# Warming products, the order of small ACT and PE steps, and units of four columns in a fused dynamic convolution and maxout kernel

## The chip, the cores and the metric

The kernel runs on one core of a Trainium2 chip (trn2). The metric is the device time of one execution in microseconds (us). Engines are named as the profile names them: PE is TensorE (PEld its weight loads), DVE is VectorE, ACT is ScalarE, POOL is GpSimd, and SP is SyncE, which only issues DMAs here. Median of four runs before the change: 415.58 us (415.46 to 415.68).

## The reference

```python
# dynamic convolution: batch 8, sequence 4160, 192 channels, 8 heads, 7 taps
w = exp(weight_gen - max); w = w / (sum(w) + 1e-9)      # over the 7 taps
x_unf = x padded by 6 zeros in front, 7 shifted views, split into heads
attn = einsum('bshk,bskhg->bshg', w, x_unf)             # 24 channels for each head
# maxout layer on the 33280 tokens
h1 = attn @ w1 ; h2 = attn @ w2                         # 192 -> 1024 each
out = maximum(h1, h2) @ w_out                           # 1024 -> 192
```

Since max(h1, h2) = h1 + relu(h2 - h1), the kernel computes `attn @ (w1 @ w_out) + relu(attn @ (w2 - w1)) @ w_out`. The small product w1 @ w_out is called w10 in the code, and w2 - w1 is `wd`.

## The kernel before

Tokens lie as 128 partitions by 260 columns: partition p holds 260 consecutive tokens, and a column is one token of each partition. Columns are worked on in batches of 16 (the last one has 4). For a batch ACT makes exp, DVE the sums over taps, ACT the logarithm, DVE subtracts it, and ACT's second exp (`weights`) gives normalized weights `en_t` in bf16. DVE multiplies (`mul`) seven shifted views of x by them into `m_t` and adds the seven products in three steps (`adds`) into `y_t`.

A unit is the columns whose features are transposed and multiplied together: four columns in the first two batches (units 0 to 7), eight after that (28 units), and a last one of four. For units 0 to 7 PE transposes and sums the taps in PSUM (`sum_transpose`, L224 on) and ACT copies the sum to `yt` (L246). For later units a DMA transpose on SP's queue does it (`transpose`, L203 on), followed on POOL by a small copy (`gate`) that waits for the transpose and so holds back the loads behind it.

There are 260 tiles, as many in a unit as it has columns. A tile of a unit of eight is one chunk of 128 hidden features for the 1024 tokens of the unit: six products with 512 columns (`hid_tile`, L264 on). A tile of a unit of four is two chunks for its 512 tokens: twelve products with 256 columns. All have 64 rows, so that two run side by side in the two halves of the array. ACT's `relu` (L283) copies a finished tile from PSUM to `rd_t`. Results are made for pairs of columns: six products with w10 (L327) and 32 with `wo` (L315). Half of these (`out_first`) can follow at once; the other half (`out_second`) writes the banks that the first one wrote, and so waits for `go`, a relay through ACT's queue (`relay`, L346). `evac` (L354) copies results to `o_t`, a ring of 24 columns, and issues or holds back the output DMA of each unit.

Tiles go in groups: eight groups of two (tiles 0 to 15), then groups of three. `hidden` (L434) writes one group's order: features of all tiles but the last, first half of some results, relus, features of the last tile, its relu, `between`, second half of the results, their evacuation. `beside` is the group's share of the softmax work and of DVE's work for later units. How many result columns a group makes is planned in advance (`OUTS`, L402 on): two and four in turn in the long run, as far as their units are complete. Results lag 9 to 10 columns behind the tiles there, and eight columns remain for `rest_of_results` (L460) at the end.

Each engine works in program order. The order of the start is written out by hand (L569 to L645): 115 and 14 warming products (`keep_warm`, L587) without use for the result, the first units, the transposes of w1, w10's product (L612) with its five copies by ACT (L628), then the calls of `hidden` from group 4 on with extra steps from `early`: a tap sum as `between` in groups 4 to 7, and in group 6 also weights and a logarithm. Softmax steps of later batches come due at given tiles (`due`); long ones are put off where the group before had one too. The PSUM buffers of the first stage are two of `hd` and two of `op`; the tap sums, the transposed w1, w10's product and the results share the two of `op`. From tile 16 on (`later_ps`) there are one of four banks for two tiles ("ab"), one of two for the third ("c"), and one for results ("r").

Of the kernel before, what the change touches and what calls it, by code (L numbers as in the profile page):

```python
# [23 lines left out]
def kernel(  # L24
# [35 lines left out]


    UNITS = []
    for b, (c0, n) in enumerate(BATCHES):
        UNITS += [(b, o + a, min(8, w)) for o, w in pieces(b) for a in range(0, w, 8)]

# [136 lines left out]

    def transpose(u):  # L203

        b, o, n = UNITS[u]
        yt = pyt.tile([P, 8 // 2 * 3 * P], BF16, name="yt", tag="yt")
        nc.sync.dma_start_transpose(
            out=yt[:, 0:n // 2 * 3 * P].rearrange("p (b t) -> p b t", t=P),
            in_=y_ts[b][:, o * D:(o + n) * D],
        )  # L210
        yt_ts[u] = yt
        while held:
            held.pop(0)()

        nc.gpsimd.tensor_copy(out=gate, in_=yt[:, 0:1])  # L215
        c = b + 1 if o == 0 else b + 2
        if o == 8 and c < NB:
            load_x(c, 0, min(8, BATCHES[c][1]))
        if o == 0 and c < NB and BATCHES[c][1] > 8:
            load_x(c, 8, BATCHES[c][1] - 8)  # L220
        if o == 0 and b + 3 < NB:
            load_wg(b + 3, nc.gpsimd)
# [44 lines left out]
    def hid_tile(t):  # L267


        u = TILES[t][0]  # L270
        fs, w = chunks(t)
        for f in fs:
            for s in range(3):
                for j in range(2):
                    nc.tensor.matmul(  # L275
                        hid_out(t, f, j), lhsT=wd[half(j), s * F + f * P:s * F + (f + 1) * P],
                        rhs=_sub(yt_ts[u][half(j), :], (s + j) % 3 * P, [[3 * P, w // P], [1, P]]),
                        start=(f == fs[0] and s == 0), stop=(f == fs[-1] and s == 2),
                        skip_group_check=True,
                    )  # L280
# [15 lines left out]
    def place(p):  # L296

        u, i, _ = column(2 * p)
        b, o, n = UNITS[u]
        return BATCHES[b][0] + o + i, n // 2  # L300

# [19 lines left out]
    def out_first(now):  # L321

        for c in now[::2]:
            u, i, _ = column(c)
            for s in range(3):
                for j in range(2):
# [26 lines left out]
    def evac(p, n):  # L353
# [3 lines left out]
        if p == NT // 2 - 1:  # L357

            for j, copy, eng in ((0, nc.scalar.copy, nc.scalar), (1, nc.vector.tensor_copy, nc.sync)):
# [6 lines left out]
            return  # L366
        runs = [[q for q in range(p, p + n) if column(2 * q)[0] == u]
                for u in range(column(2 * p)[0], column(2 * (p + n - 1))[0] + 1)]
        for qs in runs:
# [4 lines left out]
        for q in range(p, p + n):  # L374
            u, i, _ = column(2 * q)
            if u < NU - 1 and i == UNITS[u][2] // 2 - 1:
                stores.append((nc.scalar if u < 4 else nc.sync, place(q)[0] - i, [1, 2 * (i + 1) * D]))
            if u == NU - 1:
                stores.append((nc.sync, place(q)[0], [2 * D, 2], [1, D]))
        for eng, c, *ap in stores:  # L380
# [6 lines left out]

            if 4 <= u < NU - 3:
                held.append(issue)
            else:  # L390
                while u > 3 and held:
                    held.pop(0)()
                issue()
# [9 lines left out]
    for g in range(3, len(GROUPS)):  # L403
        most = 4 if g == 3 else 2 if GROUPS[g][1] == 2 or len(OUTS[-1]) == 4 else 4
        n = min(most, ready[g] - c)
        OUTS.append(list(range(c, c + n)))
# [27 lines left out]
    def hidden(g, now=(), between=lambda: None, beside=lambda: None):  # L434
# [6 lines left out]
        if now:  # L441
            out_room(now, "ab" if n == 1 and "ab" in ps else None)
            last = out_first(now)
        if len(now) > 2:
            relu(rd, t0, n - 1)
# [8 lines left out]
        relu(rd, t0 + n - 1, 1)  # L454
        between()
        if now:
            out_second(now, go)
            evac(now[0] // 2, len(now) // 2)
        if len(now) <= 2:
            beside()  # L460

    def rest_of_results(c):

        parts = [p for p in (c[:4], c[4:-2], c[-2:]) if p]
        assert max(map(len, parts)) <= 4
# [20 lines left out]
    with tc.tile_pool(name="pstage", bufs=1) as pstage:  # L486
# [100 lines left out]
        def keep_warm(times):  # L587

            for _ in range(times):
                nc.tensor.matmul(warm[:, 0:P], lhsT=ident, rhs=ident, start=True, stop=True,  # L590
                                 skip_group_check=True)

        keep_warm(115)
        w_diff(0, nc.scalar.copy)
        sum_transpose(0)
        keep_warm(14)
        mul(0, 4)

# [16 lines left out]
        def w10_product():  # L615

            pw = ps["o"].tile([P, 1024], FP32, name="pw", tag="op")
            for at, c0, nr in ((0, 0, P), (512, P, 64)):
                for fi in range(FCH):
# [3 lines left out]
                        start=(fi == 0), stop=(fi == FCH - 1), skip_group_check=True,  # L623
                    )
            for k, to, frm, at in ((0, 0, 0, 0), (1, 0, 64, 0), (2, 64, 0, 0), (1, 64, 0, 512),
                                   (2, 0, 0, 512)):
# [8 lines left out]
        weights(1, 0)  # L635
        weights(1, 4)
        mul(1, 0)
        adds(1, 0, True)
        sum_transpose(2, LEFT)
        load_x(2, 0, 16)  # L640
        load_wg(4, nc.gpsimd)
        mul(1, 4)
        hidden(3)
        w10_product()
        exp_sum(2)  # L645
# [32 lines left out]
    for c in range(3, NB):  # L678
# [8 lines left out]
        for t, *step in parts_:  # L687
            due.setdefault(t, []).append(step)
    waiting, long_in_two = [], [False]

# [13 lines left out]
    def extra(t):  # L704
# [14 lines left out]
        if s == 8 + later and b + 2 < NB:  # L719
            adds(b + 1, 8, beside=lambda i, of: red(b + 3, i, 2) if b + 3 < NB and i < 2 else None)  # L720
        if k == n // 4 - 1 and 7 < u + 1 < NU:
            transpose(u + 1)

# [53 lines left out]
```

The softmax here doesn't subtract the row's maximum and nothing guards it: scores larger than these inputs give would overflow.

## Time and profile before

| | before |
|---|---|
| median of four runs | 415.58 us |
| the profiled execution | 415.57 us |
| its span, first to last instruction | 413.8 us |
| PE busy | 397.0 us, 7369 products |
| DVE busy | 377.2 us |
| ACT busy | 359.1 us |
| POOL busy | 71.8 us |
| HBM, mean over the span | 149 GB/s |

The span is what the profile's rows cover; 1.77 us of the execution lie around it. Busy time of PE is modelled to the end of each product, and products overlap, so the distance between starts says more than a duration. In the order of time a line gives start, length, engine, line of the kernel, operation and tile, and in brackets the idle time of that engine before it and who ended it. The busiest groups, not repeated below, are the relu of two or one tiles (206 instructions, 234.4 us on ACT), result products (4160, 210.6 us on PE), feature products (1584, 187.3 us) and DVE's multiplications (37, 187.5 us).

### The profile page before, as it was taken

The page shows a single profiled execution, that of the slowest core. Times are in us where ns is not written, and L with a number is a line of the kernel's source. Part 1 is how long each engine was busy: PE and PEld are TensorE (multiplying, and loading weights), DVE is VectorE, ACT ScalarE, POOL GpSimd, SP SyncE. Part 2 cuts the span into 40 slices and gives each one's busy share as a digit, 9 for nine tenths or more (in the row PEclk, how much of TensorE's full clock was granted, in tenths as well). Part 3 has the DMA queues.
Part 4 walks back from the last instruction along what each step waited for, and adds up shares of the span by engine and source line. Part 5 has one row for each costly group of instructions (what it writes and reads, how often), then busy time and mean ns, then how long its engine had stood idle before and what let it go on. Part 6 is the DMA issues. An engine that isn't in the chain of part 4 may idle for free.

```text
span 413.8 us, 16025 instructions
## 1 busy us (share of the span) xinstructions
PE 397.0 (96%) x7369; PEld 321.9 (78%) x7369; DVE 377.2 (91%) x218; ACT 359.1 (87%) x424; POOL 71.8 (17%) x102
## 2 busy tenths in 40 slices
PE   7878899999999999999999999999999999999995
PEld 7767799777777777777777777777778777787795
DVE  5999999999999999999999999999999999999000
ACT  5888989999988999889898899998999988988771
POOL 1510101121211221220121221211221212210000
PEclk9999999999999999999999999999999999999999
DMA  8966437777566867856696588479649657643413
GB/s 238 258 169 174 109 54 184 153 178 144 167 126 144 225 157 124 222 158 118 163 215 155 119 233 165 104 182 239 131 92 257 168 56 240 157 89 115 175 58 135
DMA packets 60242, 65.68 MB, mean 159 GB/s; under 512 B 47601, under 2 KB 48497, under 8 KB 60176
## 3 DMA queue, kind: packets, MB, share of 16 engines
q1 hardware_dynamic: 51328, 38.89, 34.9%
q0 software_dynamic: 8128, 24.11, 28.7%
q10 hardware_dynamic: 720, 1.67, 1.0%
q8 instruction: 57, 0.93, 0.9%
q14 instruction: 9, 0.07, 0.1%
HBM read 35.96 MB, written 25.56 MB: 149 GB/s over the span
## 4 chain that ended last, share of the span: by engine, by line
PE 82%; ACT 8%; issue 3%; DVE 3%; DMA 2%; SPq 1%; ACTq 0%; DVEq 0%
PE op_ps L315 37%; PE hd L275 36%; PE op_ps L327 7%; ACT rd_t L285 5%; DVE m_t L173 2%; DMA ws1T<-in_moe_w_dram 2%; PE hdp L275 1%; ACT o_t L371 1%; ACT en_t L158 1%; ACT yt L246 1%; ACT e_t L127 0%; PE yps L239 0%; SPq L513 0%; PE tp L578 0%; DVE sum_t L139 0%
## 5 line engine op out<-in xcount | busy, mean ns | idle before, releaser
L285 ACT ACTIVATE rd_t<-hd 128x1024 bf16<-128x1024 f32 (+1 forms) x206 | 234.4, 1189 | 27.5 <-PE hd L275 26.0
L315 PE MATMUL op_ps<-wo,rd_t 64*128 64x192 bf16 x4160 | 210.6, 243 | 0.1
L315 PEld LDWEIGHTS <-rd_t 64*128 64x128 bf16 x4160 | 180.5, 94 | 15.7 <-ACTq L348 0.3
L275 PE MATMUL hd<-yt,wd 64*128 64x512 bf16 (+1 forms) x1584 | 187.3, 360 | 1.1 <-ACT rd_t L285 1.1
L173 DVE TENSOR_TENSOR m_t<-xb_t,en_t 128x10752 bf16<-128x10752 bf16 (+1 forms) x37 | 187.5, 5069 | 0.5 <-ACT en_t L158 0.5
L275 PEld LDWEIGHTS <-wd 64*128 64x128 bf16 x1776 | 94.4, 94 | 43.6 <-issue 3.3
L215 POOL CAST gate<-yt 128x1 f32<-128x1 bf16 x29 | 36.2, 1247 | 278.9 <-DMA yt<-y_t 278.9
L189 DVE TENSOR_TENSOR m_t<-m_t 128x4608 bf16<-128x4608 bf16 (+1 forms) x34 | 79.5, 2337 | 0.1
L371 ACT COPY o_t<-op_ps 128x384 f32<-128x384 f32 (+1 forms) x99 | 57.4, 592 | 13.1 <-PE op_ps L315 13.0
L327 PE MATMUL op_ps<-w,yt 64*128 64x192 bf16 x780 | 55.5, 243 | 3.8 <-ACT w L628 1.8
L327 PEld LDWEIGHTS <-yt 64*128 64x128 bf16 x780 | 38.4, 94 | 20.8 <-issue 5.4
L195 DVE TENSOR_TENSOR m_t<-m_t 128x3072 bf16<-128x3072 bf16 (+1 forms) x29 | 49.9, 1721 | 0.1
L158 ACT ACTIVATE en_t<-wg_t 128x896 bf16<-128x896 f32 (+2 forms) x45 | 35.0, 817 | 0.0
L198 DVE TENSOR_TENSOR y_t<-m_t 128x1536 bf16<-128x1536 bf16 (+1 forms) x29 | 27.3, 940 | 0.5
L361 DVE COPY o_t<-op_ps 128x192 f32<-128x192 f32 x1 | 0.4, 356 | 26.0 <-ACT o_t L361 26.0
L147 DVE TENSOR_TENSOR wg_t<-wg_t,sum_t 128x280 f32<-128x280 f32 (+4 forms) x45 | 21.9, 488 | 1.7 <-ACT sum_t L142 1.6
L139 DVE TENSOR_REDUCE sum_t<-e_t 128x64 f32<-128x448 f32 (+2 forms) x30 | 19.4, 648 | 2.5 <-ACT e_t L127 2.5
L115 POOL DMA_DIRECT2D xb_t<-in_x_dram x32 | 17.2, 537 | 23.8 <-DVE m_t L173 16.1
L127 ACT ACTIVATE e_t<-wg_t 128x896 f32<-128x896 f32 (+1 forms) x17 | 16.0, 940 | 2.9 <-DMA wg_t<-in_weight_gen_dram 2.5
L285 ACT ACTIVATE rd_t<-hdp 128x1024 bf16<-128x1024 f32 x16 | 15.8, 1029 | 1.5 <-PE hdp L275 0.5
L275 PE MATMUL hdp<-yt,wd 64*128 64x256 bf16 x192 | 13.2, 269 | 1.3 <-ACT yt L246 1.1
L590 PE MATMUL warm<-ident 128*128 128x128 bf16 x129 | 9.9, 253 | 3.0 <-DVE ident L529 3.0
(45 smaller groups left out, 80.2 us busy)
## 6 DMA issues: line engine op xcount, KB each, us to landing
out_dram<-o_t SPq DMA_DIRECT2D x28, 768.0 KB, 4.6
xb_t<-in_x_dram POOLq DMA_DIRECT2D x28, 384.0 KB, 5.1
wg_t<-in_weight_gen_dram POOLq DMA_DIRECT2D x14, 448.0 KB, 6.4
xb_t<-xb_t POOLq DMA_DIRECT2D x16, 288.0 KB, 5.5
out_dram<-o_t ACTq DMA_DIRECT2D x4, 384.0 KB, 2.7
out_dram<-o_t SPq DMA_DIRECT2D x4, 384.0 KB, 5.3
wg_t<-in_weight_gen_dram SPq DMA_DIRECT2D x2, 448.0 KB, 5.4
xs<-in_x_dram SPq DMA_DIRECT2D x2, 384.0 KB, 6.6
```

Of the source, the lines that this page charges most:

```text
L147: nc.vector.tensor_tensor(out=w_t, in0=w_t, in1=_sub(s_ts[b], hs.start, [[1, hs.stop - hs.start], [0, K]]), op=ALU.subtract)
L158: nc.scalar.activation(out=_sub(en_ts[b], (o * WGC + j * N * K) * 2, [[2 * N, K], [2, N], [1, 2]]), in_=_sub(wg_ts[b], (o * H + j * N) * K ...
L173: nc.vector.tensor_tensor(out=m_out, in0=x_in, in1=_sub(en_ts[b], o * WGC * 2, [[2, K * n * H], [0, G // 2], [1, 2]]), op=ALU.mult,)
L189: nc.vector.tensor_tensor(out=taps(0, 1, 3), in0=taps(0, 1, 3), in1=taps(3, 1, 3), op=ALU.add)
L195: nc.vector.tensor_tensor(out=taps(0, 2, 2), in0=taps(0, 2, 2), in1=taps(1, 5, 2), op=ALU.add)
L198: nc.vector.tensor_tensor(out=_sub(y_ts[b], o * D, [[64, 2], [P, 3 * w // 2], [1, 64]]), in0=taps(0, 1, 1), in1=taps(2, 1, 1), op=ALU.add,)
L215: nc.gpsimd.tensor_copy(out=gate, in_=yt[:, 0:1])
L275: nc.tensor.matmul(hid_out(t, f, j), lhsT=wd[half(j), s * F + f * P:s * F + (f + 1) * P], rhs=_sub(yt_ts[u][half(j), :], (s + j) % 3 * P, ...
L285: nc.scalar.activation(out=rd[:, k * 1024:(k + n) * 1024], in_=hd[:, at:at + n * 1024], func=AF.Relu)
L315: return nc.tensor.matmul(op_out(c), lhsT=rd[half(r), k * 1024 + at:k * 1024 + at + P], rhs=wo[half(r), f * D:(f + 1) * D], start=False, s ...
L327: nc.tensor.matmul(op_out(c + j), lhsT=yt_ts[u][half(j), (3 * i + (s + j) % 3) * P:(3 * i + (s + j) % 3 + 1) * P], rhs=w10[half(j), s * D: ...
L371: nc.scalar.copy(out=_sub(o, c % 24 * D, [[D, len(qs)], [h * D, 2], [1, D]]), in_=_sub(tile_, at + (qs[0] - p) * D, [[D, len(qs)], [512, 2 ...
```

## The change

1. The warming products become 20 and 2 products of 512 columns, which read the same identity four times over.
2. Group 3 is written out: its two tiles' features, w10's product, the relu of tile 6, w10's copies, the weights of columns 20 to 23 (which stood before the DVE product of columns 16 to 19), then the relu of tile 7.
3. In `hidden` the call of `between` comes after the second half of the results and their evacuation.
4. From batch 7 on (column 112) a unit has four columns, while the DMA transpose still takes eight: `piece` gives for a unit the eight columns it belongs to and which half of them it is. Their tiles have two chunks and 256 columns. Outputs are still stored by eight columns, and transposes are asked for at the same tiles as before (`MOVES`).
5. From column 112 on a group makes four columns whenever the results lag by more than six (or seven) columns. That gives four groups of four in a row (groups 40 to 43), then two and four in turn; results lag 6 to 7 columns behind, and four columns remain for the end.

```diff
+    HALVES = 7
     UNITS = []
     for b, (c0, n) in enumerate(BATCHES):
-        UNITS += [(b, o + a, min(8, w)) for o, w in pieces(b) for a in range(0, w, 8)]
+        UNITS += [(b, o + a, 4 if b >= HALVES else w) for o, w in pieces(b)
+                  for a in range(0, w, 4 if b >= HALVES else w)]
+
+    def piece(u):
+
+        b, o, n = UNITS[u]
+        return (b, o - o % 8, dict(pieces(b))[o - o % 8], o % 8 // 4) if b >= HALVES else (b, o, n, 0)
...
-    def transpose(u):
-
-        b, o, n = UNITS[u]
+    def transpose(us):
+
+        b, o, n, _ = piece(us[0])
...
-        yt_ts[u] = yt
+        for u in us:
+            yt_ts[u] = yt
...
-                        rhs=_sub(yt_ts[u][half(j), :], (s + j) % 3 * P, [[3 * P, w // P], [1, P]]),
+                        rhs=_sub(yt_ts[u][half(j), :], (piece(u)[3] * 6 + (s + j) % 3) * P, [[3 * P, w // P], [1, P]]),
...
-            if 4 <= u < NU - 3:
+            if 4 <= u < NU - 5:
                 held.append(issue)
...
         most = 4 if g == 3 else 2 if GROUPS[g][1] == 2 or len(OUTS[-1]) == 4 else 4
+        if GROUPS[g][0] >= 16 * HALVES and GROUPS[g][0] - c > (6 if GROUPS[g][0] < 16 * HALVES + 24 else 7):
+            most = 4
...
-        if len(now) > 2:
+        if len(now) > 2 and n > 1:
             relu(rd, t0, n - 1)
...
         relu(rd, t0 + n - 1, 1)
-        between()
         if now:
             out_second(now, go)
             evac(now[0] // 2, len(now) // 2)
+        between()
...
-        parts = [p for p in (c[:4], c[4:-2], c[-2:]) if p]
+        parts = [p for p in (c[:-2][:4], c[:-2][4:], c[-2:]) if p]
...
-                nc.tensor.matmul(warm[:, 0:P], lhsT=ident, rhs=ident, start=True, stop=True,
-                                 skip_group_check=True)
-
-        keep_warm(115)
+                nc.tensor.matmul(warm[:, 0:512], lhsT=ident, rhs=_sub(ident, 0, [[0, 4], [1, P]]),
+                                 start=True, stop=True, skip_group_check=True)
+
+        keep_warm(20)
         w_diff(0, nc.scalar.copy)
         sum_transpose(0)
-        keep_warm(14)
+        keep_warm(2)
...
         weights(1, 0)
-        weights(1, 4)
         mul(1, 0)
         adds(1, 0, True)
         sum_transpose(2, LEFT)
         load_x(2, 0, 16)
         load_wg(4, nc.gpsimd)
+        rd = room(3)
+        for t in (6, 7):
+            hid_tile(t)
+        pw = w10_product()
+        relu(rd, 6, 1)
+        w10_copies(pw)
+        weights(1, 4)
         mul(1, 4)
-        hidden(3)
-        w10_product()
+        relu(rd, 7, 1)
...
+    MOVES = []
+    for u in range(8, NU):
+        if piece(u)[3] == 0:
+            us = [v for v in range(u, NU) if piece(v)[:2] == piece(u)[:2]]
+            MOVES.append((us, TILES.index((u, 0)) - (4 if u == 8 else 7)))
...
-        if k == n // 4 - 1 and 7 < u + 1 < NU:
-            transpose(u + 1)
+        for us, at in MOVES:
+            if t == at:
+                transpose(us)
```

More of the change, by code (lines that the diff above doesn't have):

```diff
@@ L298, in place @@
         u, i, _ = column(2 * p)
-        b, o, n = UNITS[u]
-        return BATCHES[b][0] + o + i, n // 2
+        b, o, n, h = piece(u)
+        return BATCHES[b][0] + o + 2 * h + i, n // 2
     def op_out(c):
@@ L324, in out_first @@
             u, i, _ = column(c)
+            i += 2 * piece(u)[3]
             for s in range(3):
@@ L366, in evac @@
             return
-        runs = [[q for q in range(p, p + n) if column(2 * q)[0] == u]
-                for u in range(column(2 * p)[0], column(2 * (p + n - 1))[0] + 1)]
+        of = {q: piece(column(2 * q)[0])[:2] for q in range(p, p + n)}
+        runs = [[q for q in of if of[q] == at_] for at_ in dict.fromkeys(of.values())]
         for qs in runs:
@@ L375, in evac @@
             u, i, _ = column(2 * q)
-            if u < NU - 1 and i == UNITS[u][2] // 2 - 1:
+            _, _, w, h = piece(u)
+            i += 2 * h
+            if u < NU - 1 and i == w // 2 - 1:
                 stores.append((nc.scalar if u < 4 else nc.sync, place(q)[0] - i, [1, 2 * (i + 1) * D]))
@@ L624, in w10_product, with w10_copies @@
                     )
+            return pw
+        def w10_copies(pw):
             for k, to, frm, at in ((0, 0, 0, 0), (1, 0, 64, 0), (2, 64, 0, 0), (1, 64, 0, 512),
```

## The prediction

> **What bounds the kernel now.** I read the page first, then stage sums, the order of time where TensorE (PE) idles, and last the features' landings. Busy time of the page:
>
> ```profile
> PE 397.0 (96%) x7369; PEld 321.9 (78%) x7369; DVE 377.2 (91%) x218; ACT 359.1 (87%) x424; POOL 71.8 (17%) x102
> ```
>
> Three engines are near full, so shares decide nothing; stages do (columns: engine busy us and count in the order PE, PEld, DVE, ACT, POOL):
>
> ```profile
> 3.00:8.00 5.00, 5.00 (x48) 5.00 (x49) 2.17 (x3) 2.20 (x3) 0.00 (x0) 1.00 1.03 320
> 8.00:12.00 4.00, 3.96 (x74) 3.79 (x73) 3.54 (x4) 3.02 (x10) 1.05 (x2) 1.00 1.05 309
> 36.00:53.00 17.00, 15.23 (x450) 14.35 (x446) 17.00 (x9) 15.51 (x22) 1.06 (x2) 1.00 0.37 98
> 53.00:73.00 20.00, 20.00 (x434) 20.00 (x432) 19.97 (x14) 18.14 (x22) 1.74 (x3) 1.00 0.57 128
> 113.00:383.00 270.00, 269.61 (x4682) 210.18 (x4680) 268.49 (x148) 242.12 (x270) 51.77 (x65) 1.00 0.68 160
> ```
>
> From 53 us on PE does not pause: time lost before 53 us, or PE work added after it, reaches the end. DVE is as full, with its own order, and idles after 384. In 36 to 53 PE lacks 1.8 us. The order of time there:
>
> ```profile
> 32.32 0.42 PE L327 MATMUL op_ps<-w,yt 64*128 64x192 bf16 x6 [1.83 <-ACT w L628]
> 36.10 0.31 ACT L142 ACTIVATE sum_t<-sum_t 128x128 f32<-128x128 f32 x1 [1.09 <-DVE sum_t L139]
> 44.92 0.42 PE L327 MATMUL op_ps<-w,yt 64*128 64x192 bf16 x6 [0.77 <-ACT yt L246]
> 47.61 1.02 ACT L158 ACTIVATE en_t<-wg_t 128x896 bf16<-128x896 f32 x1
> 48.73 0.78 ACT L246 CAST yt<-yps 128x768 bf16<-128x768 f32 x1
> 49.41 0.49 ACT L371 COPY o_t<-op_ps 128x384 f32<-128x384 f32 x1
> 49.56 0.42 PE L327 MATMUL op_ps<-w,yt 64*128 64x192 bf16 x6 [0.89 <-ACT yt L246]
> 51.34 1.02 ACT L285 ACTIVATE rd_t<-hdp 128x1024 bf16<-128x1024 f32 x1 [0.52 <-PE hdp L275]
> 52.48 0.72 PE L275 MATMUL hd<-yt,wd 64*128 64x256 bf16 x10
> ```
>
> The reader is to see that PE's results wait for the ACT copy of the tap sum (`yt`), since that copy frees the PSUM buffer first, and that ACT then idles 0.52 us for the tile that PE did late. The last line is where the first three-tile group starts.
>
> The later steady state and its nearest limit:
>
> ```profile
> 306.94 0.84 PE L315 MATMUL op_ps<-wo,rd_t 64*128 64x192 bf16 x16
> 307.60 0.83 PE L275 MATMUL hd<-yt,wd 64*128 64x512 bf16 x6
> 308.25 0.84 PE L315 MATMUL op_ps<-wo,rd_t 64*128 64x192 bf16 x16
> 308.96 0.39 PE L275 MATMUL hd<-yt,wd 64*128 64x512 bf16 x2
> 314.76 0.34 POOL L215 CAST gate<-yt 128x1 f32<-128x1 bf16 x1 [10.86 <-DMA yt<-y_t]
> ```
>
> Sixteen result products take 0.66 us (306.94 to 307.60), but 0.71 before the next group's features: 0.05 us of waiting for relu in every two groups. The gate copy at 314.76 waits for the transpose that PE uses from 314.7 (tile 200, second of a pair begun at 314.03): there DVE's features come just in time, so PE could not be earlier.
>
> **The change part by part.** The sum is against the profiled run: span 413.8 us, 415.57 us in all, so 1.77 us lie around the span; it is 0.01 under the median, 415.58.
>
> *Warming.* 129 products of 128 columns become 22 of 512. The two first stage rows give 5.00/48 = 0.104 and 3.96/74 = 0.054 us for one, so 0.42 and 0.21 us for a long one. From 3.0 to 7.9, where the rate changes, 11 to 12 run, the other 8 or 9 take 1.9 us: done near 9.7 instead of 11.9. Nothing starts earlier, since the tap sum behind them starts at 11.95, when the DVE product that began at 8.94 ends (11.90). Gain 0 to 0.05; take 0. New are 2.2 us without PE work before 11.95 and 1.6 instead of 1.05 before 15.29. Idle stretches of 1.83 and 2.06 us in this trace were followed by products at full rate, so I take no loss; the other bound is the fall in clock priced below. The Trainium skill ("TensorE: Matmul & The Clock Gate", Part 1) says that the array falls back to half rate after an idle window of about 3.4 us and that warming is a matter of time, not of products; by it these gaps cost nothing either, while the trace took 4.9 us to warm, not 3.4.
>
> *w10's copies between relus.* ACT order now: w1t copies to 27.16, four weights of 0.3, `yt` 0.7, two relus 1.8, five copies 1.5 (from 30.72). After: two weights, `yt`, relu 6, copies (from 29.2, done by 30.8), two weights (done by 31.4), relu 7. PE's first results start near 30.9 instead of 32.32, 1.4 us earlier. But the ACT work is the same, and the ln at 36.10 waits for DVE (1.09 us), whose order is unchanged; evacuation and relu 8 queue behind it on ACT. So 1.4 us on PE are worth 0 at 36.1. DVE's mul(1,4), which starts at 32.12, needs the moved weights: 0.7 us to spare. If that cover went, DVE would slip by what is missing, and the ln with it; 0 to +0.3.
>
> *Tap sums behind results.* Now the evacuation frees the buffer first. From 37.57 ACT steps by 0.92 per relu, 0.68 per `yt`, 0.37 per evacuation, 0.92 per weights, 0.2 per ln, a store issue 0.4. In the new order: relu 10 at 42.2 as before, relu 11 at 43.1, evacuation 44.0, store, `yt` 44.95, relus 45.6 and 46.6, evacuation 47.5 (done 47.95), weights, ln, `yt` 48.95, relu 14 at 49.6. PE's results start at 48.15 after tile 14 instead of 49.56, tile 15 is done by 49.7, so relu 15 follows relu 14 at 50.5 instead of 51.34, and the three-tile stage starts at 51.7 instead of 52.48: **-0.8 us**. Bounds: 0 (ACT has hardly idle time here) and -1.3 (all that PE gets ahead at 48.15 is kept). The weights and ln of tile 12's group are now behind an evacuation: the ln ends near 49.1 instead of 48.83, and DVE needs it at 53.19. SP and POOL issue nothing in these steps.
>
> *Units of four from column 112.* 144 tiles take twelve products of 256 columns instead of six of 512: 864 more products, and weight loads with them. Tiles 16 to 31 already do so, and there the starts of every second group's results lie 8.63 and 8.62 us apart (57.33, 65.96, 74.58); with 512 columns 8.64 (122.16, 130.80, 139.44). Each tile is 0.655 instead of 0.648, 0.045 us in six tiles, but the 0.05 wait goes, as the shorter product ends sooner for relu. 24 times -0.02 to 0: **-0.1**. The Trainium skill ("TensorE: Matmul & The Clock Gate", Back-to-back issue gap) speaks against it: with its fixed 2.5 ns per product, an estimate of 144 x 3 pairs x 2.5 ns is +1.1 us, and with that in place of the row the sum would end at 415.8.
>
> Three consecutive groups more give four columns; the lag of results falls from 9 or 10 columns to 6 or 7. That moves 3 columns x 0.78 us (19 pairs of products x 0.0825 for two) = 2.35 us of PE work ahead of the later features, so at tile 200 PE comes 1.5 us later relative to DVE even after a gain of 0.8: the gain is kept. Without this it would be given back at 314.7. Output stores, which SP issues behind transposes, land at least 6.7 us before their ring of 24 columns is rewritten, so earlier evacuations do not wait. Transposes stay at the same tiles on SP, with POOL's gate and loads behind them; the rest of the bookkeeping gives the same stores for the same columns.
>
> *Softmax steps on ACT.* The two-column groups change places, so the groups with two weights (rows at 258 and 328, behind which PE loses 0.18 and 0.21 us) are split, while one pairs exp with weights: -0.4 to +0.2; take **-0.3**. An ln near 266.5 has 0.5 us before DVE needs it; a slip there moves features by 0.3 at most, under the 1.5 to spare.
>
> *End.* Four columns in place of eight remain. PE work is the same, but the last pair's buffer is that of the four columns just before: their evacuation (0.3 wait + 0.80, behind the last relu) ends about 2.45 us after the last features, PE comes at 2.23: **+0.3** (0 to 0.5). What follows PE's end, 4.8 us, stays.
>
> Sum: 413.8 - 0.8 - 0.1 - 0.3 + 0.3 = 412.9, with 1.77 around it 414.6 to 414.7; take **414.6**.
>
> **Rivals.** *A. ACT stays the bound before 53 us*, and only the waiting is exchanged. For it: 15.51 us of 17 busy, and store issues besides. Against: the 0.52 idle before 51.34 is ACT's own. Then 415.57 - 0.1 - 0.3 + 0.3 = 415.4; the same if features come late after all.
>
> *B. Slower: PE's instructions arrive late.* At 22.16 PE idled 2.06 us with nothing named, while a 16 KB packet of its instruction queue had started only at 19.85. From column 112 on a packet would be used up in 5.9 us instead of 7.4 (372 loads and products per two groups, not 300). One such stall: 414.6 + 2.1 = 416.7; it decides from 1.8 us lost. Against: between 53 and 73 us the density is the same and PE is busy 20.00 of 20.00.
>
> *C. The clock falls back after the shorter warming.* From 15.29 on PE work of 4.1 us would double; ACT's two idle stretches (1.14 before 23.64, 1.09 before 36.10) hide 2.2; at worst +1.7: 416.3.
>
> **How the numbers follow.** Forecast 0.60, its own range 414.0 to 415.0 from the bounds above; A 0.22; B 0.10; C 0.08. Faster by over 0.2% (about what a measurement of this kernel can tell, 0.83 us, under 414.75): 0.51, all from the forecast, 0.09 of which falls short. Within: 0.09 + 0.22 + half of C = 0.35. Slower: B and half of C, 0.14. The range 414.0 to 415.9 holds the forecast, A and a part of C.
>
> **What would show it.** Right: the first results near 30.9, yet ln still at 36.1; PE waiting for `o_t` copies, not `yt`; the three-tile stage at 51.7; 8.63 us per two groups after 124 us without the 0.05 wait; no PE wait for a landing near tile 200; a pause of 0.3 us before the last pair. Wrong: a PE wait named "issue" after 53 us, first products after 13 us at 0.107 us, or ACT's relu 15 still at 51.3.

## The result and the profile after

The change takes 416.51 us (median of 33 executions, 416.03 to 418.26); the kernel before takes 415.68 us on the same chips (median of 51, 415.24 to 417.45). The ratio is 1.0014, 95% interval 1.0007 to 1.0021: slower, though by less than the 0.2% that the prediction took as what a measurement can tell, where 414.6 us was forecast. Of the 51 executions of before, 13 are 0.9 us or more above the median of the others, 415.57 us, so that the ratios show less of a loss than the spans of the profiled executions. The profiled execution took 416.5 us with a span of 414.7 us, 0.9 us more than the 413.8 of before and 1.8 more than the forecast's 412.9.

The page's busy times after the change (time, share of the span, instructions):

```profile
PE 396.7 (96%) x8126; PEld 360.6 (87%) x8126; DVE 377.3 (91%) x218; ACT 359.6 (87%) x423; POOL 76.1 (18%) x102
```

The same stages as in the prediction, after the change (us; then busy us and count of PE, PEld, DVE, ACT, POOL; granted clock, DMA share, GB/s):

```profile
3.00:8.00 5.00, 4.99 (x12) 1.80 (x13) 2.04 (x2) 2.25 (x3) 0.00 (x0) 1.00 1.03 321
8.00:12.00 4.00, 2.26 (x15) 0.83 (x15) 3.70 (x4) 3.06 (x10) 1.20 (x2) 1.00 1.05 314
36.00:53.00 17.00, 14.76 (x430) 13.72 (x425) 17.00 (x9) 15.66 (x22) 1.06 (x2) 1.00 0.38 101
53.00:73.00 20.00, 19.91 (x429) 19.61 (x427) 19.97 (x14) 18.18 (x21) 1.26 (x3) 1.00 0.49 126
113.00:383.00 270.00, 268.80 (x5466) 251.22 (x5463) 264.88 (x146) 239.74 (x267) 54.67 (x64) 1.00 0.65 158
```

The last row matters. Between 113 and 383 us DVE is busy 264.88 us where it was 268.49, and PE 268.80 where it was 269.61, though PE has more products to do. DVE, whose work did not change, lost 3.6 us to waiting. The rows of waits say for what. First before, then after (engine, tile and line that waited, what it waited for: us in all, times, longest):

```profile
DVE wg_t L147 <- ACT sum_t L142: 1.6, 3, 0.8
```

```profile
DVE wg_t L155 <- ACT sum_t L150: 5.4, 5, 2.3
PE hd L284 <- DMA yt<-y_t: 1.0, 2, 0.7
```

DVE's subtraction (L155) waits for ACT's logarithm (`ln`, L150), and further on PE waits for transposed features, which it never did before. Two logarithms in the order of time, those of batches 10 and 11; the first line is the start of the group of tiles in which the first of them is due (tile 130). Before:

```profile
213.56 1.47 PE L275 MATMUL hd<-yt,wd 64*128 64x512 bf16 x12
...
217.33 0.34 ACT L142 ACTIVATE sum_t<-sum_t 128x128 f32<-128x128 f32 x1
219.75 0.44 DVE L147 TENSOR_TENSOR wg_t<-wg_t,sum_t 128x280 f32<-128x280 f32 x1
...
243.24 0.35 ACT L142 ACTIVATE sum_t<-sum_t 128x128 f32<-128x128 f32 x1
243.62 0.45 DVE L147 TENSOR_TENSOR wg_t<-wg_t,sum_t 128x280 f32<-128x280 f32 x1
...
250.01 1.43 SPq L207 DMA_TRANSPOSE yt<-y_t  x1
```

After, with the first wait for features that comes of it:

```profile
216.28 1.49 PE L284 MATMUL hd<-yt,wd 64*128 64x256 bf16 x24
...
220.59 0.50 ACT L381 COPY o_t<-op_ps 128x384 f32<-128x384 f32 x1
220.95 0.34 ACT L150 ACTIVATE sum_t<-sum_t 128x128 f32<-128x128 f32 x1
221.33 0.45 DVE L155 TENSOR_TENSOR wg_t<-wg_t,sum_t 128x280 f32<-128x280 f32 x1 [1.94 <-ACT sum_t L150]
...
246.97 0.34 ACT L150 ACTIVATE sum_t<-sum_t 128x128 f32<-128x128 f32 x1
247.35 0.45 DVE L155 TENSOR_TENSOR wg_t<-wg_t,sum_t 128x280 f32<-128x280 f32 x1 [2.27 <-ACT sum_t L150]
...
253.72 1.43 SPq L215 DMA_TRANSPOSE yt<-y_t  x1
...
317.02 0.83 PE L284 MATMUL hd<-yt,wd 64*128 64x256 bf16 x12 [0.72 <-DMA yt<-y_t]
```

Before, these logarithms ended 2.08 us and 0.03 us before DVE took them up. After, they start 3.62 and 3.73 us later on ACT. DVE comes to the first of them 0.44 us earlier than before (its multiplication ahead of it starts at 213.64 instead of 214.08) and stands for 1.94 us; it is 1.58 us late at the second one, for that wait, and stands for another 2.27 us. The next transpose is late by 3.7 us (253.72 against 250.01). PE then lacks 0.21, 0.89 and 0.45 us at 281.9, 316.8 and 352.4, by the distances of its products' starts against those of undisturbed groups: 1.55 us.

The start of the change went much as forecast until 51.63 us:

```profile
30.79 0.42 PE L337 MATMUL op_ps<-w,yt 64*128 64x192 bf16 x6 [0.69 <-ACT w L646]
36.06 0.31 ACT L150 ACTIVATE sum_t<-sum_t 128x128 f32<-128x128 f32 x1 [1.09 <-DVE sum_t L147]
51.63 1.49 PE L284 MATMUL hd<-yt,wd 64*128 64x256 bf16 x24 [0.40 <-ACT rd_t L294]
52.36 0.80 ACT L255 CAST yt<-yps 128x768 bf16<-128x768 f32 x1 [0.41 <-ACT o_t L381]
53.21 0.56 PE L337 MATMUL op_ps<-w,yt 64*128 64x192 bf16 x6
```

The three-tile stage starts at 51.63 instead of 52.48. The last tap sum's copy (`yt`), now behind an evacuation and a store issue, ends at 53.16, and the first results of the three-tile stage need its buffer: 0.27 us of PE at 53.21. With 0.08 more nearby, 0.47 us of 0.85 is left (tile 32 starts at 73.47 instead of 73.94).

The later steady state, and the end:

```profile
305.46 0.83 PE L284 MATMUL hd<-yt,wd 64*128 64x256 bf16 x12
306.11 0.84 PE L324 MATMUL op_ps<-wo,rd_t 64*128 64x192 bf16 x16
306.80 1.49 PE L284 MATMUL hd<-yt,wd 64*128 64x256 bf16 x24
...
408.64 2.16 PE L324 MATMUL op_ps<-wo,rd_t 64*128 64x192 bf16 x48
...
411.62 0.34 SPq L372 DMA_DIRECT2D out_dram<-o_t  x1
```

From 306.11 to 306.80 are 0.69 us for sixteen result products of 0.66: the wait of one in two groups is still there, 0.04 us in the median. Two groups now take 8.673 us (median distance of the starts of first results two groups apart, 255 to 383 us) where they took 8.636.

The accounts, after against before, in us of the profiled executions: start -0.47; 24.8 pairs of groups at +0.037, +0.92; pauses of PE at softmax steps -0.75 (0.36 left of 0.39, 0.18, 0.33 and 0.21); features late +1.55; a new pause before the last pair +0.16; together +1.41, while the last 48 result products start at 408.64 instead of 407.08, +1.56. From there to the end of the span are 6.06 us instead of 6.72, -0.66. Sum +0.9.

### The profile page after: what moved, and what is told of

Same layout as the page of the kernel before. It is cut to its first block, busy times and chain, and to the rows that moved or that the text cites. A ratio compares the mean times of both kernels' runs of the same rounds, so it can differ in the third digit from the quotient of the medians.

```text
span 414.7 us, 17539 instructions
## 1 busy us (share of the span) xinstructions
PE 396.7 (96%) x8126; PEld 360.6 (87%) x8126; DVE 377.3 (91%) x218; ACT 359.6 (87%) x423; POOL 76.1 (18%) x102
## 3 DMA queue, kind: packets, MB, share of 16 engines
q10 hardware_dynamic: 720, 1.67, 1.1%
## 4 chain that ended last, share of the span: by engine, by line
PE 54%; DVE 28%; ACT 9%; issue 5%; DMA 3%; SPq 1%; ACTq 0%; DVEq 0%
PE op_ps L324 25%; PE hd L284 24%; DVE m_t L181 14%; ACT rd_t L294 6%; DVE m_t L197 5%; PE op_ps L337 5%; DVE m_t L203 4%; DMA ws1T<-in_moe_w_dram 2%; DVE sum_t L147 2%; ACT o_t L381 1%; DVE y_t L206 1%; DVE wg_t L155 1%; ACT en_t L166 1%; DMA yt<-y_t 1%; ACT yt L255 1%
## 5 line engine op out<-in xcount | busy, mean ns | idle before, releaser
L284 PE MATMUL hd<-yt,wd 64*128 64x256 bf16 (+1 forms) x2448 | 189.2, 290 | 2.3 <-ACT rd_t L294 1.3
L284 PEld LDWEIGHTS <-wd 64*128 64x128 bf16 x2640 | 140.9, 94 | 23.7 <-issue 8.4
L224 POOL CAST gate<-yt 128x1 f32<-128x1 bf16 x29 | 40.5, 1395 | 278.2 <-DMA yt<-y_t 278.2
L155 DVE TENSOR_TENSOR wg_t<-wg_t,sum_t 128x280 f32<-128x280 f32 (+4 forms) x45 | 22.0, 488 | 5.4 <-ACT sum_t L150 5.4
L604 PE MATMUL warm<-ident 128*128 128x512 bf16 x22 | 7.8, 526 | 3.0 <-DVE ident L543 3.0
```

What stands on the lines that cost most here:

```text
L284: nc.tensor.matmul(hid_out(t, f, j), lhsT=wd[half(j), s * F + f * P:s * F + (f + 1) * P], rhs=_sub(yt_ts[u][half(j), :], (piece(u)[3] * 6 ...
```

## The experiments

Two theories came out of the comparison. *Dues*: the planning rule for more results from column 112 on (the two lines with `most = 4`) moves work of PE and ACT ahead of each later tile, three columns or 2.35 us in the mean; the logarithms are due at tiles and go with them, DVE does not; so DVE waits. *Columns*: products of 256 columns cost PE 0.04 us in two groups more by themselves. Rivals: features are late because DVE or the DMA is slower, not because of the logarithms; the gain at the start is void; the clock.

### Which part delays the features

Run ln puts the logarithms of batches 8 to 16 earlier, by two tiles (about 3 us) or four; all else is as in the change.

```diff
-            ln_at = -2 if c == 4 else 0 if c < 8 else 2 if c < 11 else 4
+            ln_at = -2 if c == 4 else 0 if c < 14 or c == 16 else 2
```

> The changed kernel with the logarithms of batches 8 to 16 due one or two groups earlier. Theory (features late): in the changed kernel DVE waited 0.43, 1.94 and 2.27 us for three logarithms, since their tiles come later there; all features after them came up to 4 us late and PE waited 1.5 us for them (at 281.9, 316.8 and 352.4). Then these DVE waits fall under 0.5 us in sum, the transpose for tile 160 starts near 249.7 instead of 253.72, the three PE waits go, and the time falls by 1.2 to 1.6 us, to some 415.0. Rival (units of four alone): DVE had time to spare, PE is slowed by its own smaller products, and the time moves by less than 0.4 us.

Measured: 415.08 us (10 executions, 414.74 to 415.53), ratio to before 0.9970 [0.9959, 0.9982], 1.4 us less than the change. The same steps in its trace:

```profile
215.75 0.29 ACT L150 ACTIVATE sum_t<-sum_t 128x128 f32<-128x128 f32 x1
...
219.10 0.44 DVE L155 TENSOR_TENSOR wg_t<-wg_t,sum_t 128x280 f32<-128x280 f32 x1
...
242.77 0.44 DVE L155 TENSOR_TENSOR wg_t<-wg_t,sum_t 128x280 f32<-128x280 f32 x1
```

DVE waits for neither, the transpose of 253.72 starts at 249.14, and PE waits for features nowhere; they land at least 2.9 us before they are used. So the features were late for the late logarithms, and not for a slower DVE or DMA; with them in time the kernel is 1.4 us faster, about the 1.55 that PE had waited.

Run norule takes out the planning rule alone.

```diff
-        if GROUPS[g][0] >= 16 * HALVES and GROUPS[g][0] - c > (6 if GROUPS[g][0] < 16 * HALVES + 24 else 7):
-            most = 4
```

> The changed kernel without the rule that shortens the lag: units of four from column 112, results 9 to 10 columns behind as before. Theory (features late): tiles keep their places among the results, so the logarithms come in time and DVE waits under 1 us; what is left is 0.04 us in two groups for the units of four (8.676 instead of 8.638, 0.9 us in all), less 0.47 from the start, and up to 0.4 us of waiting for features near tile 200: span 414.2 to 414.6, time 416.0 to 416.4. Rival (units of four alone): as the changed kernel, 416.5.

Measured: 415.65 us, ratio 0.9990 [0.9980, 1.0001], span 413.6. Its row of waits for the logarithms, all of the execution:

```profile
DVE wg_t L155 <- ACT sum_t L150: 1.4, 4, 0.4
```

In the second half DVE waits twice for 0.34 us, the transpose starts at 249.49, and PE does not wait for features, though they land only 0.16 us early at tile 224. The rule that moves the tiles is therefore what makes the logarithms late. The time is below the 416.0 to 416.4 of its theory, which had allowed for waits for features that did not come, and far below its rival's 416.5. The benefit of the rule is real too: run ln has 3 us of room at tile 224 where norule has 0.16. PE comes to that tile 1.79 us later (350.83 against 349.04), and the rest is features that land earlier.

Run halves leaves the units of four and the rule and undoes the three edits of the start; run early is the reverse, the start alone with units of eight.

```diff
# halves: warming, group 3 and `between` as before the change
# early:
-    HALVES = 7
+    HALVES = 99
...
-            if 4 <= u < NU - 5:
+            if 4 <= u < NU - 3:
```

> Only the units of four and the shorter lag; warming, w10's copies and tap sums as before the change. Theory (features late): PE starts 0.47 us later than in the changed kernel, but the logarithms come later too, so DVE still waits over 4 us and the features set the time: 416.4 to 417.0. Rival (units of four alone): the time is that of the changed kernel plus 0.47, about 417.0, with DVE waits that cost nothing.

> Only the start of the change (warming, w10's copies, tap sums behind results); all later units have eight columns and results lag as before. Both theories: the three-tile stage starts 0.85 us earlier, of which 0.35 is lost at once to the wait at 52.9. Theory (features late): 0.47 us remain, but features for tile 200 were just in time before, so about 0.4 of it is given back at 314 us; span 413.6 to 413.8, time 415.4 to 415.6. Rival: the 0.47 us are kept, 415.1.

Measured: halves 417.23 us, 1.0030 [1.0018, 1.0042]; early 416.71 us, 1.0007 [0.9990, 1.0024]. In halves DVE waits 0.84, 1.95 and 2.27 us for the logarithms, in early 0.29 once. So the loss is there without the edits of the start. Halves is a little above the numbers of its theory and of its rival and does not tell these two apart; ln and norule do. Early missed both of its numbers. In it the features bind a little later all the same: PE waits 0.81 us for them at 348.5 (tile 224), which is more than the 0.5 us that the start had given. Early's span of 415.3 also holds 1.5 us at the very end: its last 48 products start at 407.01 us, before the change at 407.08. That is told in the last section; the median of early therefore does not price the start.

### The parts of the start, with the logarithms out of the way

These three undo one edit of the start each in run ln; run ln2 is run ln once more on other chips.

```diff
# lnbetw: the tap sums ahead of the results again
         relu(rd, t0 + n - 1, 1)
+        between()
         if now:
             out_second(now, go)
             evac(now[0] // 2, len(now) // 2)
-        between()
# lnw10: group 3 as before the change, product of w10 and its copies behind both relus
         weights(1, 0)
+        weights(1, 4)
...
-        weights(1, 4)
         mul(1, 4)
-        relu(rd, 7, 1)
+        hidden(3)
+        w10_copies(w10_product())
# lnwarm: 115 and 14 warming products of 128 columns
-        keep_warm(20)
+        keep_warm(115)
...
-        keep_warm(2)
+        keep_warm(14)
```

> Run ln with the tap sums ahead of the results again. Theory of the prediction: three-tile stage starts 0.8 us later (52.7 instead of 51.9), and of this the 0.5 us that was left in the changed kernel after 57 us shows in the time: 415.6. Rival (the early gain is used up by later waits for features): 415.1, the same as run ln.

> Run ln with w10's copies and the weights before them in the order from before the change (product behind both relus). Theory of the prediction (TensorE's first results come 1.4 us later, 32.2 instead of 30.8, but the ln at 36.1 waits for DVE either way): the three-tile stage starts where it does in run ln, time within 0.2 us of it. Rival (the gain at the three-tile stage needs both reorderings): stage 0.5 us or more later, 415.5.

> Run ln with the long warming back (129 products of 128 columns, TensorE busy to 11.9 us). If the short warming's two idle stretches let the clock fall to half (as the profile of run ln shows from 13.3 to 20.2 us) and this costs time: granted clock 1.0 from some 8 us on, no half stretch, results and features at the start earlier, time 0.3 us or more below run ln's 415.08. If the fall is hidden behind ACT and DVE as the first results suggest: no half stretch, but the same time within 0.2 us.

> Run ln once more, beside run split, for the price of the short warming. If the fall of the clock to half in some executions costs time, its executions spread by clock: those with a granted clock of 0.991 take longer than those at 1.0 by 0.3 us or more. If not: 415.1, the two kinds alike within 0.2 us.

Measured: ln2 414.93 us (0.9969 [0.9956, 0.9982]); lnbetw 415.56 (0.9984 [0.9967, 1.0002]); lnw10 414.83 (0.9970 [0.9955, 0.9985]); lnwarm 414.78 (0.9971 [0.9955, 0.9986]). The tap sums behind the results are worth 0.5 to 0.6 us, the 0.47 that was left in the changed kernel's trace and a little more; in lnbetw PE waits for the copy of the tap sum as it did before the change:

```profile
49.49 0.42 PE L337 MATMUL op_ps<-w,yt 64*128 64x192 bf16 x6 [0.90 <-ACT yt L255]
...
52.41 1.49 PE L284 MATMUL hd<-yt,wd 64*128 64x256 bf16 x24
```

w10's copies are worth nothing: in lnw10 the first results come 2.0 us later than in the change and in ln2, and the time is that of ln2.

```profile
32.78 0.42 PE L337 MATMUL op_ps<-w,yt 64*128 64x192 bf16 x6 [1.83 <-ACT w L646]
```

The short warming makes no difference in the ratios to before: 0.9970 and 0.9969 in ln and ln2, 0.9971 in lnwarm. By the medians lnwarm is 0.15 to 0.3 us the faster (414.78 against 414.93 and 415.08, each on another chip), so that a price of that size is not excluded. The clock is told of in the last section.

### What the columns cost

Two prices of 0.04 to 0.05 us in two groups are mixed here: that of the 256-column products themselves, and the wait for a relu that comes late. The first attempt to part them issued, in groups with two result columns, the first tile's relu right behind its products.

```diff
# lnrelu, on run ln
         for t in range(t0, t0 + n - 1):
             hid_tile(t)
+            if n > 2 and len(now) == 2:
+                relu(rd, t, 1)
...
             for t in range(t0, t0 + n - 1):
-                relu(rd, t, 1)
+                if not (n > 2 and len(now) == 2):
+                    relu(rd, t, 1)
```

> The change with the two-wait ln dues of run ln, and in three-tile groups with two columns of results the first tile's relu is now issued right behind that tile's products, so that it waits for its own tile and not for the second one. Theory (the 0.044 us before the next group's features is relu of the first tile coming late, since TensorE signals only the second tile's end): two groups from column 112 on take 8.63 us instead of 8.676 and those before 8.59 instead of 8.64; over some 24 and 8 pairs of groups that is 1.0 to 1.5 us of TensorE, and features have 2.9 us to spare in run ln, so it is kept: 413.6 to 414.1 against 415.08 of run ln. Rival (the 0.04 is the price of the 256-column products themselves, or ACT is full and the later relus come as late as before): 8.67 stays, 415.1.

Measured: 472.1 us, ratio 1.135 [1.132, 1.138]. Both theories missed it. Its trace, PE first, and its row of waits:

```profile
285.68 0.83 PE L284 MATMUL hd<-yt,wd 64*128 64x256 bf16 x12
287.69 0.83 PE L284 MATMUL hd<-yt,wd 64*128 64x256 bf16 x12 [1.17 <-ACT rd_t L294]
```

```profile
PE hd L284 <- ACT rd_t L294: 53.4, 43, 2.0
```

The two tiles share one buffer of four banks. With the relu between them in program order, the second tile's products wait for the relu that reads the first tile, although it reads other banks: 43 waits and 53.4 us in all. So the two tiles seem to be tied together by the buffer. Run split therefore gives each its own buffer of two banks (the relu over two tiles, 1.88 us, becomes two of 1.02); it starts from lnwarm.

```diff
-        for k in ("ab", "c", "r"):
+        for k in ("a", "b", "c", "r"):
...
-            ab = ps["ab"].tile([P, 2048], FP32, name="hd2", tag="ab")
             for t in range(t0, t0 + n - 1):
-                hd_at[t] = ab, (t - t0) * 1024
+                k = "ab"[t - t0]
+                hd_at[t] = ps[k].tile([P, 1024], FP32, name="hd_" + k, tag=k), 0
...
-        if len(now) > 2 and n > 1:
-            relu(rd, t0, n - 1)
-        else:
-            for t in range(t0, t0 + n - 1):
-                relu(rd, t, 1)
+        for t in range(t0, t0 + n - 1):
+            relu(rd, t, 1)
```

> Run lnwarm (two-wait ln dues, long warming) with the PSUM buffer of a group's first two tiles split into two buffers of one tile each, so that every relu is one of 1024 columns and waits for, and frees, its own tile alone; in four-column groups the relu over two tiles (1.88 us) becomes two of 1.02. Theory (the wait of 0.044 us before the next group's features is the first tile's relu waiting for the second tile, because the two share one buffer): from column 112 on two groups take 8.63 instead of 8.676 us, over some 32 pairs of groups 1.0 to 1.5 us, and features have 2.9 us to spare: 413.3 to 413.8 against 414.78. Rival (ACT, which gets 0.16 us more in two groups, is the limit): 8.67 or more, 414.8 or above.

Run split8 is the same with units of eight throughout, and run ln8 has units of eight, the short warming and the shared buffer; both have the logarithms of batches 8 and 11 two tiles earlier.

```diff
-    HALVES = 7
+    HALVES = 99
...
-            ln_at = -2 if c == 4 else 0 if c < 8 else 2 if c < 11 else 4
+            ln_at = -2 if c == 4 else 0 if c < 9 else 2 if c < 12 else 4
```

> The same split buffers with units of eight columns throughout, the ln of batches 8 and 11 earlier, long warming. If the 0.04 us that units of four add in two groups is the price of 256-column products by themselves, two groups after column 112 take 8.59 us here against 8.63 in run split, and the difference stays when the relu wait has gone. If it came from the relu wait, both are 8.59. On TensorE alone this would be 1 us less than run split; but features, with at most 0.9 us to spare at tile 224 in run ln8, take most of it back: 413.7 in an execution whose last store is not held up. Rival (features wait for DVE from the start of the second half): 414.6, as the better executions of run ln8.

> Only the start of the change (warming, w10's copies, tap sums behind results), units of eight columns throughout, and the ln of batches 8 and 11 put earlier. Theory (the start is worth 0.5 us on TensorE, and without the four-column units neither the 0.04 us per two groups nor late lns take it back; features are the next limit, 0.3 us earlier than in run early): DVE waits under 0.1 in sum, feature waits 0.5 instead of 0.81, span 413.0 to 413.4 in an execution whose last store is not held up, 414.8 to 415.2. Rival (DVE's own pace is the limit in this form): span 413.8, 415.6, as before the change.

Measured: split 412.56 us (412.22 to 413.58), ratio 0.9914 [0.9890, 0.9937]; split8 413.78 (413.40 to 415.52), 0.9948 [0.9931, 0.9965]; ln8 415.56 (414.54 to 417.61), 0.9992 [0.9972, 1.0012]. Split in the later steady state, and its stage row:

```profile
303.82 0.84 PE L324 MATMUL op_ps<-wo,rd_t 64*128 64x192 bf16 x16
304.48 0.83 PE L284 MATMUL hd_a<-yt,wd 64*128 64x256 bf16 x12
305.14 0.83 PE L284 MATMUL hd_b<-yt,wd 64*128 64x256 bf16 x12
```

```profile
113.00:383.00 270.00, 270.00 (x5526) 254.34 (x5522) 268.86 (x149) 245.30 (x302) 50.60 (x65) 1.00 0.68 162
```

Sixteen result products are now 0.66 us apart from the next features, and PE is busy 270.00 of 270. The periods of two groups (medians, 255 to 383 us) part the two causes:

| | units of eight (512 columns) | units of four (256 columns) |
|---|---|---|
| shared buffer | 8.636 (before) | 8.673 (change), 8.674 (ln) |
| own buffers | 8.587 (split8) | 8.632 (split) |

Across, 256 columns cost 0.045 without any wait; down, the shared buffer costs 0.04 to 0.05 with either. Split gained more than the 1.0 to 1.5 us expected, since the waits for relu at 80, 84 and 109 us (0.35, 0.28 and 0.28 of idle time in lnwarm) and a pause of 0.17 at 193 us went with it, against one new wait of 0.28 at 85.1. The 0.27 us near 53 stayed: from the first features of the three-tile stage to the first results are 1.58 us in both (51.52 to 53.10 in lnwarm, 51.54 to 53.12 in split). Whether a relu gained by waiting for its own tile or PE by writing a buffer that is free earlier is not told apart. ACT is busy 5.6 us more in the stage than in the change, and PE does not wait for it.

In split8 PE is on the features' heels, as expected, at three places of 0.31, 0.44 and 0.36 us:

```profile
312.58 0.82 PE L284 MATMUL hd_b<-yt,wd 64*128 64x512 bf16 x6 [0.44 <-DMA yt<-y_t]
```

So units of four pay with the buffers split: they cost 0.045 us in two groups, but with less lag the features land 0.43 us early at tile 224 (split), and PE never waits for them. That is not the whole of it. Split's span is 0.95 us shorter than split8's (410.63 and 411.58), and its last 48 products start only 0.35 us earlier (404.54 and 404.89); the other 0.60 lies behind them, in the shorter end that four remaining columns leave. In ln8 DVE waits for no logarithm after 100 us and PE for no features; its better executions are at 414.5 to 415.0, near its theory's 414.8 to 415.2, the others are up to 3 us longer, and the median is the rival's 415.6, without the longer span that the rival named (412.8 in the profiled execution).

## Why the prediction was wrong

*Warming, 0.* Right to within 0.3 us (runs ln, ln2 and lnwarm above). The gap before the tap sum was 1.74 us in the profiled execution, 2.2 forecast. The fall of the clock (rival C) does happen in some executions, but was not worth the 1.7 us that it was given at worst.

*w10's copies, 0.* Right: first results at 30.79 (30.9 forecast), the logarithm still at 36.06 behind DVE.

*Tap sums behind results, -0.8.* Right at 51.63 (51.7 forecast), then 0.35 us too good: the tap sum's copy was moved past the evacuation and its store issue, and the results that need its buffer next were not listed as waiting for it.

*Units of four, -0.1.* Wrong, +0.92. The failed step is "the 0.05 wait goes, as the shorter product ends sooner for relu". The row at 57 to 75 us showed a period of 8.63 with 256 columns because relu is in time there, which is 8.632, the period of 256 columns without a wait; the row with 8.64 for 512 columns included the wait. The comparison set a row without a wait against one with it and took the wait for a part of the width. From the columns alone the sum would have been 24.8 x 0.045 = +1.1. The Trainium skill ("TensorE: Matmul & The Clock Gate", Back-to-back issue gap), which the prediction set aside, gave that same +1.1 as an estimate from a fixed 2.5 ns per product. The section states this for products by themselves and says that it over-counts at large N in a stream; in these runs it does not: 0.045 us for the 18 more pairs in two groups are 2.5 ns each.

*Lag and features, 0: "the gain is kept".* Wrong, +1.55. The shift of 2.35 us was seen (at tile 200 run ln has 1.45 us of it, 1.5 forecast), and counted as room for the features, since PE comes later to them. That the softmax steps due at those tiles come later with it was left out. The step that failed is "An ln near 266.5 has 0.5 us before DVE needs it; a slip there moves features by 0.3 at most": one logarithm was looked at, and under the old place. Those of batches 10 and 11, with 2.08 and 0.03 us to spare, slipped by 3.62 and 3.73. Of this, 2.72 and 2.83 us are the later starts of their groups on PE (216.28 instead of 213.56, 242.30 instead of 239.47): 2.35 us is a mean. Two groups (41 and 43) make four columns instead of two, not three groups, and two and four change places after them, so that in these groups four columns more stand ahead of the tiles, in those between only two (tiles 133 and 151 come 1.22 and 1.33 us later). The other 0.90 us, alike for both, goes with the place in the group: before, the logarithm stood between the relus of a group with four columns, after, behind the last relu and the evacuation (220.59) of a group with two. That division was read from the order of time and not tried by itself.

*Softmax steps, -0.3.* Too small: -0.75, within a group of pauses that did vanish as described. *End, +0.3.* The pause before the last pair is 0.16, and what follows PE's end is 0.66 us shorter, since the store of eight columns before the last is issued 3.25 us ahead of the last one (408.37 and 411.62) instead of 2.1, and the last one lands after 1.7 us instead of 2.4; this was taken as unchanged.

The reading "From 53 us on PE does not pause" was not quite right either: before the change PE waits for relu at 80.8, 84.8 and 109.6 us (0.35, 0.28 and 0.28). The change left these as they were, and run split removed them. Two sums of the rivals are slightly off: A's comes to 415.5, and C's 4.1 less 2.2 to 1.9.

Put together: the forecast's -0.9 becomes +0.9 by +0.33 (start), +1.02 (units), +1.55 (features), -0.45, -0.14 and -0.66, and 0.15 that the accounts leave open. Of the rivals, B had the right time (416.7) and the wrong cause: no instruction wait of PE's beyond 0.1 us was named after 53 us. A named features coming late "after all", without the mechanism and with a price of zero beyond the lost gain. The missing rival was that an engine outside the edit, DVE, would wait for steps that are tied to the moved tiles.

## What to carry to other kernels

When a plan moves work of one engine relative to another, list everything that is tied to the moved work, not only what gains room by it: here the features gained 2.35 us in the mean, and the logarithms, due at the same tiles, came 3.6 and 3.7 us later. Compare steady rates only between rows that have the same waits; a wait of 0.05 us in two groups is a microsecond in a kernel of 400. And two tiles that shared one buffer here held each other up; splitting the buffer was worth 2.2 us, where another order with the shared buffer cost 57.

## What the runs showed of the hardware

The granted clock can fall back after less than 3 us without PE work. Run ln and run ln2, the same kernel (warming products, then the tap sum with PE's idle time before it):

```profile
3.01 6.21 PE L604 MATMUL warm<-ident 128*128 128x512 bf16 x20 [3.01 <-DVE ident L543]
12.20 1.50 PE L248 MATMUL yps<-ident,m_t 64*128 64x64 bf16 x84 [2.98 <-DVE m_t L181]
```

```profile
3.01 7.18 PE L604 MATMUL warm<-ident 128*128 128x512 bf16 x20 [3.01 <-DVE ident L543]
11.96 1.40 PE L248 MATMUL yps<-ident,m_t 64*128 64x64 bf16 x84 [1.78 <-DVE m_t L181]
```

In ln the clock rose early (6.5 us), so the twenty products ended at 9.2 and PE stood for 2.98 us; from 13.3 us on the granted clock is one half for 6.8 us:

```profile
13.30:20.10 6.80, 5.93 (x124) 4.58 (x117) 6.66 (x8) 5.88 (x8) 2.65 (x5) 0.50 1.26 222
```

In ln2 it rose at 8.5 and stayed. Over the profiled executions with the short warming, gaps of 2.88, 2.95 and 2.98 us at this place (early, lnw10, ln) were followed by the fall, those of 1.43 to 2.51 us (norule, change, ln2, lnbetw, ln8, lnrelu) were not. The length of the gap is not all of it. In lnrelu the clock was at one half from 54.9 to 58.3 us too, after a wait of only 1.67 us. By the clock records of these traces, every fall came a whole number of stretches of 3.41 us after the rise: 6.52 and 13.35 us in ln, 5.98 and 12.80 in early, 6.93 and 13.76 in lnw10, 7.12 and 54.91 in lnrelu. In the stretch just before the fall PE was busy for 0.34, 0.29, 0.41 and 0.44 of the time. That is no sharp threshold, as two stretches of 0.43 in lnrelu were followed by none; but it suggests that how a gap lies in these stretches counts. No run varies that by itself. The Trainium skill ("TensorE: Matmul & The Clock Gate", Part 1) puts the fall at an idle window of about 3.4 us; here gaps of 2.88 us, and once of 1.67, were enough. The fall costs little at the start, probably because ACT and DVE set the time there: the four executions of ln2 with a mean clock of 0.991 took 414.72, 414.72, 414.91 and 415.24 us, the six with 1.00 took 414.69 to 415.10.

The other surprise is the end. In run early the last stores landed late: the store of 768 KB issued at 407.87 took 5.0 us to land, where the one issued at 407.94 before the change took 3.3, and the last one landed at 413.94. From 405 to 414 us the queues of early hold one packet that those of before do not (queue: packets, MB, share of 16 engines; then the store):

```profile
q8 instruction: 1, 0.02, 0.6%
...
out_dram<-o_t SPq DMA_DIRECT2D x1, 768.0 KB, 5.0
```

A 16 KB packet of the instruction queue began at 409.2 us, in the middle of the store. The change's own trace has one at 406.8 us, before its store of 768 KB was issued at 408.37, and that store landed after 3.2 us. This would fit the executions of before, early, ln8 and others that are 1.3 us or more longer than the rest, but the late landing was seen in this one profile, and its cause was not tried.
